# Attention output moved on chip to the expert products, and a new order for the first products

## The chip, the cores and the metric

The kernel runs on one core of one Trainium2 chip. The metric is the device time of one execution in microseconds (us), the median of the runs; lower is better. A core has TensorE (PE in the rows; its weight loads are PEld), VectorE (DVE), ScalarE (ACT), GpSimd (POOL), SyncE (SP) and 16 DMA engines. Each engine takes its instructions in the order in which the program lists them, and waits on semaphores for those of the others.

## The reference

Three stages follow each other. A delta-rule attention with a state of 48 x 48 for each of 4 x 8 heads goes over 768 tokens; its output, for 3072 tokens of 384 features, goes through 8 experts, all of which compute all tokens, weighted by a router whose weights are balanced by 8 Sinkhorn steps; a gated network with a 1024 x 1024 layer and an output layer ends it.

```python
# attention, per batch b and head h, over t
k_n = k / (norm(k) + 1e-6)
y[t] = q[t] @ state
state = state + beta[t] * outer(k_n[t], v[t] - k_n[t] @ state)
# experts; x is y as (3072, 384)
P = exp(x @ w_gate - max)
for _ in range(8):
    P /= P.sum(1) + 1e-9; P /= P.sum(0) + 1e-9; P *= N / E
out = sum_e P[:, e] * (relu(x @ w1[e]) @ w2[e])
# last network
((out @ m2_w1) * (out @ m2_w2)) @ m2_w3 @ m2_w_out
```

## The kernel before

The attention is worked in 12 chunks of 64 tokens for all 32 heads at once, 16 groups side by side on 128 partitions (two halves of 64, of which a feature-major tile like kt uses 48 rows). For each pair of chunks a triangular system is inverted on VectorE (`invert`, many short steps of lines L450, L651 and L663), from Gram products of the keys (`prep_k`, tile kt) that are copied to tile a0 and transposed (L637). For chunks 0 and 1 only the 16 x 16 blocks are inverted, and the rest is done by three corrections on TensorE (`substitute` makes R and tt; in `seq` the products of vs and tt, then three times R times u). `seq` carries the state from chunk to chunk (tiles u, st) and gives the chunk's output in xst; its feature-major form x, in two parts for exact fp32 products, is tile xr, which has two slots. `xload` brings it there: xst is written to xs_d in DRAM, read back into xst with features on 128 partitions, copied by ScalarE (line L443) into part 0 of xr, and the remainder by VectorE or GpSimd (L450) into part 1. From xr follow the router's logits (xr times wg) and the first expert's products (`e0`: xr times wA, then hA times wA, 72 products each for a chunk of 256 columns). After the last chunk come the Sinkhorn steps, and then the seven other experts (`phase_b`), which read xs_d again, and the last network (`phase_c`).

No order of instructions is written by hand. Each operation is recorded with its possible engines, a planned duration, what it reads and writes, and a priority (lower goes first); `Plan.order` then simulates the engines with these costs and fixes the order, and on which engine an operation runs where there is a choice. `room` gives buffers and PSUM banks, with a limit by class (attn 4 of 8). For TensorE there is a rule on fetching instructions: the planner reckons that a block of 256 instructions is ready `FETCH` = 4.4 us after the block before it was begun, and passes by an operation that would stand still for that. A random generator with a seed passes some attention operations by. Until the first expert product is planned, TensorE gets filler from 20 us on where nothing else can run: products of a zero tile wz (`fill`), which nobody reads. `lead` in the code is the next filler operation, and None once the filler is over. All loads and stores of this part are issued on SP's queue, which is in order too.

The loads at the start have priorities near -20, in the order kT of chunk 0 (with 16 rows of padding in each half, 512 KB), masks, kn of chunk 0, beta, kT and kn of chunk 1. Operations of chunk 0's chain have priorities of -131 to -129, those of the later chunks about -100, the first expert's products 200 and more.

```python
# xload before: one read back from DRAM, then the split
self.dma(raw, lambda: self.T["xs_d"][c].rearrange("h (k p) t -> p (h k) t", p=128), 393216, r, rk, pr, eng=q, lat=XLAT)
g.op({"ACT": act(768)}, lambda e: self.copy("ACT", dst(0), raw()), r=rk, w=[k(0)], prio=pr)
```

## Time and profile before

| what | value |
|---|---|
| runs | 1990.87, 1994.67, 1998.92 us |
| median | 1994.67 us |
| profiled execution | 1995.27 us, of which the span of the profile is 1993.5 us |
| TensorE busy | 1959.9 us (98%), granted clock 0.998 over the span |
| VectorE, ScalarE, GpSimd busy | 1576.1, 1043.6, 754.9 us |
| first product of xr and wA | 60.14 us |
| last copy of x into xr | 366.92 us |

The profile is one execution. TensorE's busy time holds the filler products, so it is read together with the rows of tile wz. The timeline merges instructions of one line that follow each other: the first number is the start, the second the length, and the brackets give the idle time before the group and what ended it.

### The profile page before, as it was taken

To read this page: it belongs to the slowest core of one execution; us is meant where nothing else is said; L and a number is where in the kernel's file an instruction comes from. 1 tells how busy PE (TensorE), PEld (TensorE's weight loads), DVE (VectorE), ACT (ScalarE), POOL (GpSimd) and SP (SyncE) were. 2 spreads that over 40 slices of the span, in tenths; PEclk is the share of its full clock that TensorE was granted. 3 is DMA by queue.
4 is the path that set the end of the run, shared out by engine and by line. 5 is a ranking of instruction groups with operands and counts; after the bars stand their busy time and mean duration, and the time that the engine had idled before them with its cause. 6 is when DMAs were issued, how large, how long until landed. Compare 5 with 4: busy or idle time off the path is not lost.

```text
span 1993.5 us, 41202 instructions
## 1 busy us (share of the span) xinstructions
PE 1959.9 (98%) x16054; PEld 1673.8 (84%) x16054; DVE 1576.1 (79%) x2753; ACT 1043.6 (52%) x2043; POOL 754.9 (38%) x964
## 2 busy tenths in 40 slices
PE   7999999999999999999999999999999999999999
PEld 6898889988888888888888888888888888888888
DVE  7989893588888787887788788888876776677875
ACT  6545433356555455544355455555554453676764
POOL 1201010457777666624433324334344533023310
PEclk9999999999999999999999999999999999999999
DMA  6443422266655565699999989999999989447341
GB/s 220 152 140 112 124 80 68 96 203 249 220 216 191 196 222 187 211 286 270 284 307 240 245 242 231 278 283 256 263 284 263 292 246 216 141 140 196 110 152 41
DMA packets 189636, 406.19 MB, mean 204 GB/s; under 512 B 16192, under 2 KB 112384, under 8 KB 175616
## 3 DMA queue, kind: packets, MB, share of 16 engines
q0 software_dynamic: 45792, 196.10, 36.8%
q1 hardware_dynamic: 143648, 207.45, 31.6%
q8 instruction: 126, 2.06, 0.4%
q14 instruction: 70, 0.57, 0.1%
HBM read 259.21 MB, written 144.28 MB: 202 GB/s over the span
## 4 chain that ended last, share of the span: by engine, by line
PE 86%; DVE 6%; DMA 4%; issue 2%; ACT 2%; POOL 1%; SPq 0%; POOLq 0%; ACTq 0%; DVEq 0%
PE b L439 86%; DMA wA<-wv_d 2%; DMA kt<-in_kT 1%; ACT rt L443 1%; DVE prod L450 1%; DVE b L450 1%; POOL xf_d L470 1%; DMA rt<-wo_d 0%; DVE p L453 0%; DMA rt<-w_d 0%; DVE hA L453 0%; DVE t L663 0%; DVE hB L453 0%; DVE acc L450 0%; DVE p L450 0%
## 5 line engine op out<-in xcount | busy, mean ns | idle before, releaser
L450 DVE TENSOR_TENSOR b<-b,rt 128x512 f32<-128x512 f32 x810 | 539.3, 694 | 104.3 <-ACT rt L443 99.8
L443 ACT ACTIVATE rt<-b 128x512 f32<-128x512 f32 x756 | 443.0, 603 | 314.6 <-PE b L439 241.8
L439 PE MATMUL b<-xT,wA 128*128 128x512 f32 x2028 | 518.6, 391 | 0.8 <-ACT rt L443 0.3
L439 PE MATMUL b<-hB,wA 128*128 128x512 f32 x1764 | 445.1, 390 | 4.3 <-DMA wA<-wv_d 1.6
L439 PEld LDWEIGHTS b<-xT,wA 128*128 128x128 f32 x2028 | 379.3, 188 | 79.9 <-DVE b L450 2.9
L439 PE MATMUL b<-hA,wA 128*128 128x512 f32 (+1 forms) x2124 | 441.8, 348 | 0.0
L439 PEld LDWEIGHTS b<-hB,wA 128*128 128x128 f32 x1764 | 330.4, 188 | 76.5 <-ACT hA L1267 4.1
L439 PEld LDWEIGHTS b<-hA,wA 128*128 128x128 f32 x2124 | 346.0, 189 | 51.3
L439 PE MATMUL b<-xr,wA 128*128 128x256 f32 (+1 forms) x1362 | 255.4, 326 | 0.8 <-DVE tt L450 0.5
L439 PEld LDWEIGHTS b<-xr,wA 128*128 128x128 f32 x1362 | 201.8, 190 | 21.8 <-DVE tt L450 0.7
L439 PE MATMUL b<-wS,wA 128*128 128x512 f32 x684 | 184.4, 391 | 0.4 <-ACT rt L443 0.3
L453 DVE SCALAR_TENSOR_TENSOR hA<-b,hA 128x512 fp32r<-128x512 f32 x188 | 126.9, 684 | 38.4 <-ACT hA L979 30.2
L470 POOL DMA_DIRECT2D xf_d<-acc x109 | 97.4, 896 | 139.7 <-DVE acc L450 106.2
L439 PEld LDWEIGHTS b<-wS,wA 128*128 128x128 f32 x684 | 127.7, 188 | 26.6 <-ACT rt L443 1.9
L450 DVE TENSOR_TENSOR tmp<-b,pb 128x512 f32<-128x512 f32 x129 | 89.1, 691 | 76.0 <-PE b L439 67.6
L453 DVE SCALAR_TENSOR_TENSOR hB<-b,hB 128x512 fp32r<-128x512 f32 x196 | 131.1, 686 | 3.0 <-ACT hB L1267 2.3
L1267 ACT ACTIVATE hB<-b 128x512 fp32r<-128x512 f32 x196 | 116.3, 603 | 21.6 <-PE b L439 14.7
L450 POOL TENSOR_TENSOR acc<-acc,tmp 128x512 f32<-128x512 f32 x78 | 102.3, 1312 | 45.5 <-DVE wA L450 20.8
L470 POOL DMA_DIRECT2D wA<-wf_d x56 | 31.7, 566 | 199.7 <-PE b L439 192.0
L1267 ACT ACTIVATE hA<-b 128x512 fp32r<-128x512 f32 x140 | 82.3, 610 | 39.6 <-PE b L439 36.0
L450 DVE TENSOR_TENSOR acc<-b,pb 128x512 f32<-128x512 f32 x81 | 55.9, 690 | 43.0 <-PE b L439 41.7
L470 POOL DMA_DIRECT2D xf_d<-tmp x65 | 57.2, 880 | 84.8 <-DVE tmp L450 49.4
(265 smaller groups left out, 2363.3 us busy)
## 6 DMA issues: line engine op xcount, KB each, us to landing
wA<-wf_d POOLq DMA_DIRECT2D x56, 1280.0 KB, 8.7
wA<-wv_d POOLq DMA_DIRECT2D x56, 768.0 KB, 8.7
wf_d<-wA SPq DMA_DIRECT2D x27, 1280.0 KB, 5.0
wA<-wc_d POOLq DMA_DIRECT2D x24, 1280.0 KB, 6.1
xf_d<-acc POOLq DMA_DIRECT2D x109, 256.0 KB, 5.5
wv_d<-wA SPq DMA_DIRECT2D x28, 768.0 KB, 4.1
xf_d<-tmp POOLq DMA_DIRECT2D x65, 256.0 KB, 5.6
yr<-in_moe_w SPq DMA_DIRECT2D x60, 192.0 KB, 2.5
```

The lines of the kernel that those rows point to most:

```text
L439: self.nc.tensor.matmul(*args, skip_group_check=True, **kw)
L443: self.nc.scalar.activation(out=out, in_=in_, func=AF.Copy, **({} if scale is None else {"scale": scale}))
L450: return self.E[eng].tensor_tensor(out=out, in0=in0, in1=in1, op=op)
L453: self.nc.vector.scalar_tensor_tensor(out=out, in0=in0, scalar=scalar, in1=in1, op0=op0, op1=op1)
L470: return self.g.op({eng: cost}, lambda _: e.dma_start(out=out(), in_=in_(), **({} if accum is None else {"accum_op": accum})), r=r, w=w, p ...
L1267: g.op({"ACT": actb(512)}, lambda e, s=s, hv=hv: nc.scalar.activation(out=hv(0), in_=self.ps(s, 512), func=AF.Relu), r=[s], w=[(o, 0, 0)], ...
```

## The change

`xload` no longer reads xs_d. Six transfers (`XMOVE`) take x from xst straight into part 1 of xr, and it is split in place; for chunk 0 three of the six are issued on ACT's queue. So that each transfer moves whole rows, the features lie in another order on the partitions: 96 of each 128 rows are two heads' features as they come, and the fourth pair of heads is spread over rows 96 to 127 of the three blocks. The rows of the gate and of the first expert's w1 are put in the same order before the launch. xs_d is still written, for the later experts, after the transfers in the program's order. kT and qT are loaded without the padding rows, each in two transfers, and the loads of chunks 0 and 1 stand in another order. In the planner, other attention products wait after 27 us (`HOLD`) until chunk 0's (`first`) are planned, the attention may hold two more PSUM banks before 44 us (`OPEN`), the fetch rule and the passing-by don't hold while filler lasts, several planned durations change, and so does the seed. Copies of chunk 1 into a0 and of chunk 0 into xst may go to VectorE. The filler products have 512 columns instead of 256, and half their number.

```diff
--- before.py
+++ after.py
@@ -37,10 +37,11 @@
-XLAT = 1.0
+XLAT = .6
+XMOVE = [(0, 0, D, 0, 0, 0, 3), (1, 0, D, D, 0, 0, 3), (0, 0, 32, 96, 0, 3, 1), (0, 32, 16, 96, 1, 3, 1), (1, 0, 16, 112, 1, 3, 1), (1, 16, 32, 96, 2, 3, 1)]
@@ -148,13 +149,15 @@
-    SEED = 79
+    SEED = 12
+    HOLD = 27.0
+    OPEN = 44.0
@@ -168,7 +171,9 @@
+        first = [o for o in self.ops if "PE" in o.engs and o.prio[0] <= -129 and o.ins >= 16]
+            o.end = None
@@ -245,7 +250,7 @@
-                if s.cls in g.caps and g.used.get(s.cls, 0) + need.get((g, s.cls), 0) >= g.caps[s.cls]:
+                if s.cls in g.caps and g.used.get(s.cls, 0) + need.get((g, s.cls), 0) >= g.caps[s.cls] + (2 if now < self.OPEN and s.cls == "attn" else 0):
@@ -292,6 +297,8 @@
+                if lead is not None and e == "PE" and o.ins >= 16 and now > self.HOLD and o.prio[0] > -125 and any(not x.end for x in first):
+                    continue
@@ -302,7 +309,7 @@
-                if o.low and full or e == "PE" and (fetch(o, now) > .1 or o.ins >= 16 and rng.random() < self.PASS_BY):
+                if o.low and full or e == "PE" and lead is None and (fetch(o, now) > .1 or o.ins >= 16 and rng.random() < self.PASS_BY):
@@ -466,7 +473,7 @@
-        cost = cost if eng == "SP" else 1.1
+        cost = 1.1 if eng == "POOL" else cost
@@ -491,7 +498,7 @@
-                  asys=((128, 1056), F32), t=((128, 1056), F32), prod=((128, NP, 1024), F32), xs=((128, 256), F32), bm2=((128, 2, 32), F32), wz=((128, 384), F16),
+                  asys=((128, 1056), F32), t=((128, 1056), F32), prod=((128, NP, 1024), F32), xs=((128, 256), F32), bm2=((128, 2, 32), F32), wz=((128, 640), F16),
@@ -504,7 +511,7 @@
-            self.dma(lambda nm=nm: T[nm], lambda src=src: a[src], 65536, [], [nm], -20.05 + i * .1)
+            self.dma(lambda nm=nm: T[nm], lambda src=src: a[src], 65536, [], [nm], -19.7 - i * .05)
@@ -536,8 +543,8 @@
-        for _ in range(400):
-            g.op({"PE": .107}, lambda e: self.mm(self.ps(sw, 256), T["wz"][:, 0:128], T["wz"][:, 128:384], start=True, stop=True),
+        for _ in range(200):
+            g.op({"PE": .214}, lambda e: self.mm(self.ps(sw, 512), T["wz"][:, 0:128], T["wz"][:, 128:640], start=True, stop=True),
@@ -550,9 +557,11 @@
-        self.dma(lambda: T["kn"][:, kn.at].rearrange("p g d -> p (g d)"), lambda: self.a["kn"][c], 393216, [], [kn], pr - 20 + c % 2)
+        self.dma(lambda: T["kn"][:, kn.at].rearrange("p g d -> p (g d)"), lambda: self.a["kn"][c], 393216, [], [kn], pr - 20.0 + (c % 2 if j else .1 * c), lat=0.0 if j else 1.3)
-        self.dma(lambda: T["kt"][:, k.at].rearrange("p g t -> p (g t)"), lambda: self.a["kT"][c], 524288, [], [k], pr - 20.1 + c % 2)
+        for b in range(2):
+            self.dma(lambda b=b: T["kt"][64 * b:64 * b + D, k.at].rearrange("p g t -> p (g t)"), lambda b=b: self.a["kT"][c, 64 * b:64 * b + D], 196608,
+                     [], [k if b else (k, b)], pr - 20.1 + (c % 2 if j else .25 * c), lat=0.0 if j else 1.3)
@@ -576,7 +585,7 @@
-        pg = pr if j == 0 else -120.0 + j if j > 1 else -99.5
+        pg = pr if j == 0 else -99.5 if j == 1 else -98.5 if j == 2 else -120.0 + j
@@ -594,17 +603,18 @@
+            ca = {"ACT": act(256, True), **({"DVE": dve(256)} if c == 1 else {})}
-            g.op({"ACT": act(256, True)}, lambda e, s=s, ss=ss, a0=a0: self.copy(
-                "ACT", T["a0"][:, a0.at, ss], self.ps(s, 8, 64)[:, :, 0:32], -1.0), r=[s], w=[ak], prio=pg)
+            g.op(ca, lambda e, s=s, ss=ss, a0=a0: self.copy(
+                e, T["a0"][:, a0.at, ss], self.ps(s, 8, 64)[:, :, 0:32], -1.0), r=[s], w=[ak], prio=pg)
-                g.op({"ACT": act(256, True)}, lambda e, s=s, ss=ss, a0=a0, r=r: self.copy(
-                    "ACT", T["a0"][r, a0.at, ss], self.ps(s, 8, 64)[r, :, 32:64], -1.0), r=[s], w=[ak], prio=pg)
+                g.op(ca, lambda e, s=s, ss=ss, a0=a0, r=r: self.copy(
+                    e, T["a0"][r, a0.at, ss], self.ps(s, 8, 64)[r, :, 32:64], -1.0), r=[s], w=[ak], prio=pg)
-                g.op({"ACT": act(128, True)}, lambda e, s=s, hf=hf, i=i: self.copy(
+                g.op({"ACT": act(128, True) + .08}, lambda e, s=s, hf=hf, i=i: self.copy(
@@ -644,11 +654,11 @@
-            g.op({"DVE": dve(4 * i * i) + .12}, port=True, fn=lambda e, pv=pv, i=i: self.tt(
+            g.op({"DVE": dve(4 * i * i)}, port=True, fn=lambda e, pv=pv, i=i: self.tt(
-            g.op({"DVE": dve(4 * i * i) + .11}, lambda e, pv=pv, i=i: nc.vector.tensor_reduce(
+            g.op({"DVE": dve(4 * i * i)}, lambda e, pv=pv, i=i: nc.vector.tensor_reduce(
@@ -791,7 +801,9 @@
-        self.dma(lambda: T["qt"][:, q.at].rearrange("p g t -> p (g t)"), lambda: self.a["qT"][c], 524288, [], [q], (pr if c > 1 else 2.5 + c) - 20)
+        for b in range(2):
+            self.dma(lambda b=b: T["qt"][64 * b:64 * b + D, q.at].rearrange("p g t -> p (g t)"), lambda b=b: self.a["qT"][c, 64 * b:64 * b + D], 196608,
+                     [], [q if b else (q, b)], (pr if c > 1 else 2.5 + c) - 20, lat=0.0 if c > 1 else 1.3)
@@ -813,14 +825,18 @@
-    def xload(self, dst, raw, rk, c, r, key, pr, q):
-
-        g = self.g
-        k = (lambda i: key[0:2] + (i,) + key[2:]) if isinstance(key, tuple) else lambda i: (key, i)
-        self.dma(raw, lambda: self.T["xs_d"][c].rearrange("h (k p) t -> p (h k) t", p=128), 393216, r, rk, pr, eng=q, lat=XLAT)
-        g.op({"ACT": act(768)}, lambda e: self.copy("ACT", dst(0), raw()), r=rk, w=[k(0)], prio=pr)
+    def xload(self, dst, src, c, r, key, pr, q):
+
+        g, T = self.g, self.T
+        raw = lambda: dst(1).bitcast(F32)
+        rk = [(key, "r", i) for i in range(len(XMOVE))]
+        for i, (b, e0, n, p0, kk, j0, nj) in enumerate(XMOVE):
+            self.dma(lambda p0=p0, n=n, kk=kk, nj=nj: T["xr"][p0:p0 + n, 1, key.at, :, kk:kk + nj].bitcast(F32).rearrange("p h k t -> p h (k t)"),
+                     lambda b=b, e0=e0, n=n, j0=j0, nj=nj: src()[64 * b + e0:64 * b + e0 + n, :, 128 * j0:128 * (j0 + nj)], 1024 * n * nj,
+                     r, rk[i:i + 1], pr, eng="ACT" if b and c == 0 else q, cost=.4, lat=XLAT)
+        g.op({"ACT": act(768)}, lambda e: self.copy("ACT", dst(0), raw()), r=rk, w=[(key, 0)], prio=pr)
-             r=rk + [k(0)], w=[k(1)], prio=pr)
+             r=[(key, 0)], w=[(key, 1)] + rk, prio=pr)
@@ -836,7 +852,7 @@
-            g.op({"ACT": .8}, scale, r=[("nv", 0)], w=[vk[i // 2]], prio=1.2 + c)
+            g.op({"ACT": .95}, scale, r=[("nv", 0)], w=[vk[i // 2]], prio=1.2 + c)
@@ -917,17 +933,14 @@
-            g.op({"ACT": act(512, True)}, lambda e, hf=hf: self.copy(e, T["xst"][:, xb.at, hf], self.ps(sy[hf], 512)),
+            g.op({"ACT": act(512, True), **({"DVE": dve(512)} if c == 0 else {})}, lambda e, hf=hf: self.copy(e, T["xst"][:, xb.at, hf], self.ps(sy[hf], 512)),
+        self.xload(lambda i: T["xr"][:, i, x.at].rearrange("p h k t -> p (h k) t"), lambda: T["xst"][:, xb.at], c, [(xb, 0), (xb, 1)], x, pr + .5, XQ)
-        xk = [("xs", c, b) for b in range(2)]
-        self.xload(lambda i: T["xr"][:, i, x.at].rearrange("p h k t -> p (h k) t"),
-                   lambda: T["xst"][:, xb.at].rearrange("p h f -> p (h f)")[:, 0:768].rearrange("p (k t) -> p k t", t=128), [(xb, "x")],
-                   c, xk, x, pr + .5, XQ)
@@ -1757,12 +1770,17 @@
+    d = np.arange(DM)
+    d = np.where(d % 128 < 96, d // 128 * 96 + d % 128, 288 + d // 128 * 32 + d % 128 - 96)
+    res["moe_w_gate"] = f(res["moe_w_gate"][d])
+    res["moe_w1"] = res["moe_w1"].copy()
+    res["moe_w1"][0] = res["moe_w1"][0][d]
```

## Rows read from the trace of the kernel before

**Rows 1.** The page: busy time, share and instructions of each engine.
```profile
PE 1959.9 (98%) x16054; PEld 1673.8 (84%) x16054; DVE 1576.1 (79%) x2753; ACT 1043.6 (52%) x2043; POOL 754.9 (38%) x964
```

**Rows 2.** Busy by stretch: length, PE, PEld, DVE, ACT, POOL, clock, DMA share, GB/s.
```profile
0.00:30.00 30.00, 18.98 (x450) 16.09 (x450) 19.05 (x41) 24.19 (x75) 2.09 (x12) 1.00 0.76 284
30.00:60.10 30.10, 27.13 (x748) 23.79 (x749) 26.01 (x45) 16.73 (x39) 9.15 (x6) 0.94 0.53 157
60.10:100.00 39.90, 38.72 (x1074) 35.15 (x1073) 37.26 (x54) 19.11 (x43) 9.99 (x7) 1.00 0.42 132
100.00:300.00 200.00, 195.62 (x5209) 180.29 (x5208) 183.27 (x286) 93.53 (x219) 20.27 (x17) 1.00 0.38 114
...
420.00:1993.50 1573.50, 1562.15 (x7015) 1306.36 (x7014) 1247.33 (x2205) 845.75 (x1583) 679.43 (x893) 1.00 0.77 226
```

**Rows 3.** Busy times by stretch, TensorE's products of tile wz alone.
```profile
30.00:60.10 30.10, 13.80 (x108) 0.94 0.53 157
```

**Rows 4.** Timeline, 10 to 16 us: start, us, engine, line, operation; idle before in brackets.
```profile
10.74 1.18 ACT L443 ACTIVATE a<-b 128x256 f32<-128x256 f32 x3
...
13.98 1.91 DVE L637 STREAM_TRANSPOSE asys<-a 128x1024 f32<-128x1024 f32 x1
...
15.19 1.14 PE L439 MATMUL b<-qt,kt 48*64 48x64 f32 x33 [1.38 <-issue]
```

**Rows 5.** Timeline, 31 to 37 us: update and first correction product of chunk 0.
```profile
31.76 1.76 PE L439 MATMUL b<-vs,tt 64*64 64x48 f32 x64
...
33.73 1.09 ACT L443 ACTIVATE xst<-b 128x512 f32<-128x512 f32 x2
...
34.94 0.91 ACT L443 ACTIVATE vs<-b 128x384 f32<-128x384 f32 x2
...
36.60 2.07 PE L439 MATMUL b<-vs,xst 64*64 64x48 f32 x64
```

**Rows 6.** Timeline of VectorE, 37 to 44 us, and the same line at 95 us.
```profile
37.83 0.56 DVE L450 TENSOR_TENSOR u<-b,vs 128x384 f32<-128x384 f32 x1 [0.27 <-ACT nrm L566]
...
40.95 1.73 DVE L576 TENSOR_TENSOR bm<-bm,nrm 128x32 f32<-128x32 f32 x1
...
42.61 1.01 DVE L450 TENSOR_TENSOR u<-b,vs 128x384 f32<-128x384 f32 x2
...
95.31 0.19 DVE L576 TENSOR_TENSOR bm<-bm,nrm 128x32 f32<-128x32 f32 x1
```

**Rows 7.** Timeline, 48 to 61 us: chunk 0's x from PSUM to the first expert product.
```profile
48.87 1.08 ACT L443 ACTIVATE xst<-b 128x512 f32<-128x512 f32 x2 [6.19 <-PE b L439]
...
49.98 1.77 SPq L470 DMA_DIRECT2D xs_d<-xst  x2
...
54.82 0.38 SPq L470 DMA_DIRECT2D xst<-xs_d  x1
...
57.96 0.84 ACT L443 ACTIVATE xr<-xst 128x768 fp32r<-128x768 f32 x1 [0.16 <-DMA xst<-xs_d]
...
60.14 0.60 PE L439 MATMUL b<-xr,wA 128*128 128x256 f32 x3
```

**Rows 8.** DMA issues: queue, count, KB each, median us from issue to landing.
```profile
xst<-xs_d SPq DMA_DIRECT2D x12, 384.0 KB, 3.5
...
y_d<-yr SPq DMA_DIRECT2D x36, 128.0 KB, 2.6
```

**Rows 9.** Timeline of TensorE, 89 to 93 us.
```profile
89.75 0.69 PE L439 MATMUL b<-asys,g 32*32 32x32 f32 x32 [1.13 <-DVE hA L453]
...
91.55 0.86 PE L439 MATMUL b<-xr,wg 128*16 128x256 f32 x6
```

**Rows 10.** Timeline, 366 us: x of chunk 11 into xr.
```profile
366.92 0.85 ACT L443 ACTIVATE xr<-xst 128x768 fp32r<-128x768 f32 x1 [2.64 <-PE b L439]
```

**Rows 11.** Timeline, 413 to 434 us: the loads of pb and their first use.
```profile
413.67 0.82 SPq L470 DMA_DIRECT2D pb<-p_d  x2
...
433.89 0.68 DVE L450 TENSOR_TENSOR acc<-b,pb 128x512 f32<-128x512 f32 x1
```

## The prediction

> **What bounds the kernel now.** I read the page first, then the busy times by stretch, then the timeline of the first 60 us, the waits there, and last the places where a delay could be hidden. TensorE is busy for 98% of the span [rows 1], but that figure counts filler. By stretch [rows 2], from 420 us on it stands idle for 11.4 of 1573.5 us: what happens there is a fixed amount of work, and only its start can move. From 60.1 us to 420 us it is idle for 8.3 us of 359.9, a little everywhere. The loose time is in front: in the first 30 us TensorE is idle for 11.0 us, and between 30.0 and 60.1 us it has 27.1 us busy, of which 13.8 us are products of the zero tile wz [rows 3]. So in 30.1 us before the first expert product there are 3.0 us idle and 13.8 us of filler: 16.8 us in which TensorE does nothing that is needed. The change speaks to this stretch, because the first expert product starts at 60.14 us [rows 7] when chunk 0's x has come on chip. The second thing to see in [rows 2] is VectorE: 37.3 of 39.9 us busy between 60.1 and 100 us and 183.3 of 200 us up to 300 us. While the attention runs there are nearly two bounds, and time given to TensorE alone isn't all kept.
>
> **The change part by part**, in the order of chunk 0's chain; each term is a gain in us.
>
> *Loads.* kT and qT lose the 16 padding rows of each half: 384 KB for 512 KB, in two issues for one. Keys kn of chunk 1 now go ahead of its kT, and VectorE may take some of chunk 1's six copies into a0. Ahead of chunk 1's kT go kT0, kn0, kn1 (3 x 384 KB) where masks, beta, kT0 and kn0 went (39 + 96 + 512 + 384 KB): its last byte comes at nearly the same place (1536 for 1543 KB). So the Gram product of chunk 1 stays near, and only ScalarE's and VectorE's work between it and the transpose at 13.98 us [rows 4] can shrink. In front of it lie six copies of 0.39 us on ScalarE [rows 4]; three of them moved would be 1.2 us at the most. Between 0 and 1.2, I take 0.6.
>
> *Costs in the planner* (scale 0.95 for 0.8, masked copies +0.08, the small inversion steps without +0.12). They move no work, they change who is put in front of whom. The rows show what that was worth: the update product of chunk 0 ends at 33.52 us, but ScalarE, still at other copies, gets to the copies of R at 33.73 and to those of vs at 34.94 us, and the first correction product starts at 36.60 us [rows 5]. With the two vs copies (0.46 each) at once on two engines after 33.7 us it would start near 34.4: 2.2 us. Between 0 and 2.2, I take 1.6: the new costs say by how much the old ones fell short on ScalarE (8 x 0.15 + 12 x 0.08 = 2.2 us), and most of these operations lie ahead of the two copies.
>
> *The hold* (after 27 us no other attention product on TensorE until chunk 0's are through). VectorE finished the first half of u at 38.39 us; the second could have followed the product, which ends at 38.67 us [rows 5], at about 38.9 us, but started at 42.61, because the norm of chunks 2 and 3 was ahead of it, with two products into bm of 1.18 and 1.73 us, the last of which [rows 6] took 0.19 us at 95.31. 3.7 us were lost. The hold binds TensorE, not VectorE, so this can come back: between 0 and 3.7, I take half, 1.9.
>
> *x path of chunk 0.* The two copies into xst take 1.08 us one after the other on ScalarE; on two engines 0.6: gain 0.5. They end at 49.95 us, and x is in hand for ScalarE at 57.96 [rows 7]: 8.0 us for a write to DRAM (two issues), its landing, a read and its landing. Now three issues on SP and three on ACT's queue go side by side, straight into xr. At 0.38 us an issue [rows 7] that is 1.14 us; no row shows a transfer from SBUF to SBUF. Nearest are the same bytes at 3.5 us and y_d<-yr at 2.6 us [rows 8]; the slow end is the first xs_d write, 4.84 us from its issue to the read that waited for it, and issues at half of 1.77 us each [rows 7]. So the new path takes 3.7 to 7.5 us, 4.6 by the nearest row; gain 3.4, between 0.5 and 4.3. ACT's three issues wait for both halves of xst, and behind them on ScalarE stand the copies of the state for chunk 1; that is 1.1 us at the most for a chain which doesn't set the first expert product, and I cost it at nothing.
>
> [...]
>
> *x path of the later chunks.* Six issues on SP (2.3 us) replace a read that waited for a write; gain near 1 us each, and hidden, since the x of chunks 2 to 11 has a chunk of products ahead of it. What moves is the place: before, x waited in xst, and the copy at 366.92 us went as soon as TensorE left the slot [rows 10]; now issue, landing and copies come after that, 2.3 + 3.5 us more. The work that hides it is the other slot's expert products. For chunk 11 the router and the Sinkhorn steps come that much later; the loads of pb are issued by 414.5 us, would be there at 419.3 even with the slow 4.84 us of above, and are used first at 433.89 us [rows 11]: 14 us of room. I cost it at nothing.
>
> *The rest.* The fetch rule is off while filler lasts, the filler has 512 columns and half the instructions, the attention may hold six PSUM banks before 44 us, the seed is another: no row gives these a price of their own, and I take 0, with the fetch rule as a rival. Some 84 more issues on SP are about 32 us of a queue that waits through most of 330 us: 0. The permuted rows of the gate and of the first expert's w1 are made before the launch.
>
> **The sum.** 0.6 + 1.6 + 1.9 = 4.1 us bring chunk 0's whole chain forward, the state for chunk 1 and VectorE's work with it: kept. The 0.5 + 3.4 = 3.9 us bring forward the expert products alone. They can take the place of filler [rows 3], but at 88.6 us TensorE has run dry (1.13 us) and chunk 1's router product is at 91.55 us [rows 9]: what it did early is missing there, unless chunk 1 too is early. I keep half, 2.0. Together 6.1 us of the profiled execution's 1995.27: 1989.2. That execution is 0.6 us above the median of the runs, so against the median 1994.67 it is 1988.6 us.
>
> **Rivals.**
> *All is kept*: the hold keeps VectorE free too and chunk 1 moves with chunk 0: 2.2 + 3.7 + 3.4 + 0.5 + 0.6 = 10.4 us, 1984.3. For it: 16.8 us of useless TensorE time stand there. Against it: the two dry places of [rows 9].
> *Nothing is kept*: VectorE is the bound until 100 us, TensorE idles in front of chunks 1 and 2 for what it gained: 1993 to 1996. For it: [rows 2].
> *Fetch stalls.* At 15.19 us TensorE stood 1.38 us for nothing that the profile shows, in the midst of one operation, with 33 of its 64 products still to come [rows 4]. The chain from the substitution to the state has seven operations of 64 products and 64 weight loads, 896 instructions; with 128 in each operation and a stop every other one, four stops of 1.38 us are 5.5 us: 1994. That can eat the gain, not turn it. [...]
> *Slower, by the late start of the moves.* From chunk 2 on, x leaves xst only when the slot in xr is free, and 5.8 us more pass before its products can start. It is covered while the other slot's products (144 of them, planned at 0.36 us for three: 17 us) and the attention last. If a chunk has less than that, TensorE waits; it decides at 0.6 us a chunk over ten chunks (6.1 us eaten), and makes 2005 at 1.6 us a chunk. SP stands in its queue for that slot, and the loads of the next chunks stand behind. For it: VectorE's 92%. Against it: at 366.92 us the copy came as the last of a row of products, with much left to do.
>
> **How the numbers follow.** A measurement of this kernel can tell 0.5%, 10 us, from no change: faster is below 1984.7, slower above 2004.6. Chances: the sum, 1985 to 1992, 0.52; all kept, 1979 to 1985, 0.21; nothing kept or fetch stalls, 1992 to 1999, 0.20; late moves, above 1999, 0.07, half of it above 2004.6 and half short of it, to which I add a little for an order that turns out badly elsewhere. Faster: 0.21 and the edge of the first case, 0.27; slower 0.06; the rest, 0.67. The terms by themselves reach from 0.2 us (0.5 x path, half kept) to 11.9 us (1.2 + 2.2 + 3.7 + 0.5 + 4.3), that is 1982.8 to 1994.4. With a little of the rivals on each side the range is 1981 to 1997.
>
> **What will show it.** The first product of xr and wA starts at 49 to 54 us, not at 60.14. From the end of the copies into xst to ScalarE's copy into xr pass 4 to 5.5 us, not 8.0. The second u starts within 1 us of its product. Filler between 30 us and the first expert product falls by 4 us or more. Between 60 and 130 us TensorE has 2 us more idle than now. From 420 us to the end the length stays within 3 us, as the work there is the same. Wrong it would be if the first expert product is early and the end isn't (the give-back is whole), if TensorE waits for transfers into xr, or if idle time without a releaser grows in chunk 0's chain.

## The result, and the profile after

The kernel after takes 2021.47 us (median of 4 runs, 2018.58 to 2023.6) against 1994.79 us for the kernel before (four runs too, one more than in the table above): ratio 1.0137, 95% interval 1.0122 to 1.0152. It is 27 us slower; 6 us faster was forecast, and the range ended at 1997. The profiled execution is 2020.77 us with a span of 2019.0 us.

The busy times by stretch come first, in the order of [rows 2] (length, PE, PEld, DVE, ACT, POOL, clock, DMA share, GB/s); the last row has TensorE alone.

```profile
0.00:30.00 30.00, 14.87 (x386) 12.72 (x387) 13.79 (x33) 18.77 (x56) 2.09 (x12) 1.00 0.98 245
60.10:100.00 39.90, 36.52 (x869) 32.71 (x859) 31.58 (x44) 20.14 (x42) 12.78 (x7) 0.96 0.48 134
100.00:300.00 200.00, 187.81 (x4813) 172.25 (x4813) 166.37 (x267) 89.86 (x214) 19.78 (x18) 0.97 0.36 103
300.00:400.00 100.00, 95.32 (x1853) 88.94 (x1851) 50.17 (x81) 30.44 (x65) 5.30 (x6) 1.00 0.22 60
400.00:450.00 50.00, 48.75 (x360) 45.91 (x361) 42.00 (x88) 26.65 (x51) 35.67 (x28) 1.00 0.39 120
...
445.00:2019.00 1574.00, 1561.99 (x7015) 1.00 0.77 226
```

The reader reads it from the end. The last 7015 products of TensorE take 1574.0 us, from 445.0 us on; before, the last 7015 took 1573.5 us, from 420.0 us on [rows 2]. The tail is the same work at the same speed, and it begins 25.0 us later. All of the loss lies ahead of it. From 60.1 to 450 us TensorE is busy 36.52 + 187.81 + 95.32 + 48.75 = 368.4 of 389.9 us, idle for 21.5. Before, the rows for the same stretch are these:

```profile
300.00:400.00 100.00, 98.76 (x1423) 94.82 (x1422) 45.04 (x96) 34.96 (x71) 22.54 (x23) 1.00 0.27 83
400.00:450.00 50.00, 48.52 (x275) 42.16 (x274) 44.16 (x81) 28.79 (x54) 26.09 (x32) 1.00 0.63 210
```

With [rows 2] that is 38.72 + 195.62 + 98.76 + 48.52 = 381.6 us busy, idle for 8.3. So 13.2 us more are idle. From 60.1 us to the start of the tail, the kernel before first and after second (length, PE, clock, DMA share, GB/s):

```profile
60.10:420.00 359.90, 351.61 (x7844) 1.00 0.35 105
60.10:445.00 384.90, 363.39 (x7869) 0.98 0.33 95
```

It is nearly the same number of products, and 25.0 of the 25.5 us by which the span grew: 13.2 us of idle time (21.5 for 8.3) and 11.8 us by which TensorE is busy longer. By an estimate, at most two thirds of the second part go to the clock column: 0.96 over 39.9 us and 0.97 over 200 us are some 1.6 + 6.0 = 7.6 us of a clock that before stood at 1.00 there, if all work went in step with it. The products of xr and wA took 415 ns each (median) in the kernel after at a clock of 0.50, from 66 to 68 us, and 282 ns at 1.00, from 71 to 78 us. The first expert product comes 3.5 us later, but that is no term of its own: by 60.1 us both kernels have about as many products behind them, filler left out (1024 before, 1017 after).

The late first product is read in the timeline of the kernel after (start, us, engine, line, operation; idle before in brackets):

```profile
21.93 0.38 SPq L477 DMA_DIRECT2D wgr<-in_moe_w_gate  x1
...
31.08 0.18 DVE L523 CAST wg<-wgr 128x24 fp32r<-128x24 f32 x1 [6.76 <-DMA wgr<-in_moe_w_gate]
...
39.74 1.10 PE L446 MATMUL b<-vs,tt 64*64 64x48 f32 x64
...
41.95 2.07 PE L446 MATMUL b<-vs,xst 64*64 64x48 f32 x64
...
43.98 0.97 DVE L457 TENSOR_TENSOR u<-b,vs 128x384 f32<-128x384 f32 x2
...
50.72 1.73 DVE L585 TENSOR_TENSOR bm<-bm,nrm 128x32 f32<-128x32 f32 x1
52.37 0.55 DVE L457 TENSOR_TENSOR u<-b,vs 128x384 f32<-128x384 f32 x1
...
52.97 0.88 PE L446 MATMUL b<-u,kraw 64*48 64x48 f32 x59 [1.99 <-DVE u L457]
...
55.45 1.08 ACT L450 ACTIVATE xst<-b 128x512 f32<-128x512 f32 x2
...
56.56 3.55 SPq L477 DMA_DIRECT2D xr<-xst  x3
56.56 2.07 ACTq L477 DMA_DIRECT2D xr<-xst  x3
...
62.78 0.84 ACT L450 ACTIVATE xr<-xr 128x768 fp32r<-128x768 f32 x1 [1.07 <-DMA xr<-xst]
...
63.67 0.39 PE L446 MATMUL b<-xr,wA 128*128 128x256 f32 x1 [0.31 <-ACT xr L450]
```

The update product of chunk 0 starts at 39.74 us; before it was 31.76 [rows 5]. Chunk 0's chain is eight us late by then. VectorE stands 6.76 us in the midst of chunk 0's inversion for a load of the gate's weights, which was issued at 21.93 us and is at hand at 31.08. Behind 39.74 us the chain is faster than before: 23.9 us to the first expert product instead of 28.4.

The waits of TensorE up to the first expert product say what else was late (engine, line, for what: us in total, times, longest), after and then before:

```profile
PE b L446 <- DMA kt<-in_kT: 11.3, 7, 4.4
PE b L446 <- issue: 6.5, 4, 1.7
```

```profile
PE b L439 <- DMA kt<-in_kT: 6.7, 2, 4.6
PE b L439 <- issue: 1.4, 1, 1.4
```

Between 60 and 440 us ScalarE's copies into xr wait for the moves:

```profile
ACT xr L450 <- DMA xr<-xst: 30.2, 12, 5.6
```

TensorE itself waits there for the three engines' copies into xr for 6.6 us (0.8 for ScalarE's, 3.9 for GpSimd's, 1.9 for VectorE's), and for 4.5 us for nothing that the profile shows; before it was none and 1.1.

At the start 11.3 us of waiting are for kT, 4.6 more than before. The loads tell why: two stretches of 5 us, the kernel after in the first fence, the kernel before in the second (length, PE, clock, DMA share, GB/s).

```profile
7.50:12.50 5.00, 3.16 (x88) 1.00 1.08 197
...
17.50:22.50 5.00, 0.63 (x12) 1.00 1.04 219
```

```profile
7.50:12.50 5.00, 3.50 (x120) 1.00 1.03 406
...
17.50:22.50 5.00, 4.28 (x88) 1.00 1.05 389
```

The DMA engines are as busy in both, at a share above 1.0, and move half as much in these two stretches (from 12.5 to 17.5 us, in between, it is 349 GB/s for 412). What differs is the shape: the kernel after loads kT and qT as transfers of 48 rows, before they had 128; kn, kraw and vs have 128 in both. By the order of issue, the four transfers of qT of chunks 0 and 1 are under way here:

```profile
9.50:12.50 3.00, 2.43 (x84) 1.00 1.02 188
```

That is 188 GB/s at a share of 1.02. Why transfers into 48 rows move so much less no run shows; what the shape costs is tried below.

### The profile page after: what moved, and what is told of

It is laid out like the page before. It is cut to its first block, busy times and chain, and to the rows that moved or that the text cites. A ratio compares the mean times of both kernels' runs of the same rounds, so it can differ in the third digit from the quotient of the medians.

```text
span 2019.0 us, 41131 instructions
## 1 busy us (share of the span) xinstructions
PE 1966.5 (97%) x15933; PEld 1671.2 (83%) x15933; DVE 1571.9 (78%) x2754; ACT 1042.0 (52%) x2045; POOL 754.9 (37%) x961
## 4 chain that ended last, share of the span: by engine, by line
PE 85%; DMA 5%; DVE 4%; ACT 2%; SPq 1%; issue 1%; POOL 0%; ACTq 0%; POOLq 0%; DVEq 0%
PE b L446 85%; SPq L477 1%; DMA kt<-in_kT 1%; DMA xr<-xst 1%; DMA wA<-wv_d 1%; ACT rt L450 1%; DMA yr<-in_moe_w 1%; DVE b L457 1%; DVE hA L460 0%; DMA rt<-wo_d 0%; DMA rt<-w_d 0%; DMA qt<-in_qT 0%; DVE p L460 0%; ACT xr L450 0%; DMA kn<-in_kn 0%
## 5 line engine op out<-in xcount | busy, mean ns | idle before, releaser
L446 PE MATMUL b<-hA,wA 128*128 128x512 f32 (+1 forms) x2313 | 497.1, 352 | 5.4 <-DMA wA<-wv_d 1.8
L446 PEld LDWEIGHTS b<-hA,wA 128*128 128x128 f32 x2313 | 381.1, 189 | 68.1 <-ACT hB L1280 3.3
L446 PE MATMUL b<-hB,wA 128*128 128x512 f32 x1575 | 392.4, 389 | 0.0
L446 PEld LDWEIGHTS b<-hB,wA 128*128 128x128 f32 x1575 | 295.6, 188 | 61.4
L446 PE MATMUL b<-xr,wA 128*128 128x256 f32 (+1 forms) x1362 | 260.0, 331 | 2.2 <-issue 1.2
L446 PEld LDWEIGHTS b<-xr,wA 128*128 128x128 f32 x1362 | 206.8, 195 | 23.2 <-issue 1.5
L460 DVE SCALAR_TENSOR_TENSOR hA<-b,hA 128x512 fp32r<-128x512 f32 x209 | 140.3, 686 | 47.1 <-ACT hA L992 44.4
L1280 ACT ACTIVATE hB<-b 128x512 fp32r<-128x512 f32 x175 | 102.6, 611 | 50.3 <-PE b L446 44.9
L460 DVE SCALAR_TENSOR_TENSOR hB<-b,hB 128x512 fp32r<-128x512 f32 x175 | 117.1, 683 | 8.1 <-ACT hB L1280 7.5
L457 POOL TENSOR_TENSOR acc<-acc,tmp 128x512 f32<-128x512 f32 x78 | 103.3, 1324 | 44.7 <-DVE wA L457 20.7
L1280 ACT ACTIVATE hA<-b 128x512 fp32r<-128x512 f32 x161 | 95.8, 602 | 17.1 <-PE b L446 10.9
```

The costliest lines, as they stand in the source:

```text
L446: self.nc.tensor.matmul(*args, skip_group_check=True, **kw)
L457: return self.E[eng].tensor_tensor(out=out, in0=in0, in1=in1, op=op)
L460: self.nc.vector.scalar_tensor_tensor(out=out, in0=in0, scalar=scalar, in1=in1, op0=op0, op1=op1)
L1280: g.op({"ACT": actb(512)}, lambda e, s=s, hv=hv: nc.scalar.activation(out=hv(0), in_=self.ps(s, 512), func=AF.Relu), r=[s], w=[(o, 0, 0)], ...
```

## The experiments

Each of them was timed against the kernel before on the chip that it ran on; several chips were used, so ratios are compared and not times. Two kinds must be kept apart. In some the instructions keep the order of before or of after on every engine, so that little else than the edit changes. In the others the planner draws a new order, and the order is part of what is measured. *Idle* is TensorE's idle time from 60.1 to 450 us, summed as above; *x waits* is the time for which ScalarE's copies into xr stand waiting for a transfer, 60 to 440 us.

| kernel | order | ratio, interval | first expert product | idle | x waits |
|---|---|---|---|---|---|
| before | | 1 | 60.14 | 8.3 | 4.8 |
| after | new | 1.0137 [1.0122, 1.0152] | 63.67 | 21.5 | 30.2 |
| b_narrow | of before | 1.0025 [1.001, 1.0041] | 62.57 | 8.8 | 6.4 |
| b_movefix | of before | 1.0303 [1.0282, 1.0323] | 58.96 | 40.2 | 60.0 |
| b_move01 | of before | 1.0009 [0.9996, 1.0022] | 58.38 | 10.1 | 6.3 |
| a_wide | of after | 1.0093 [1.0066, 1.0119] | 58.77 | 20.5 | 30.3 |
| a_wgr | of after | 1.0138 [1.0105, 1.0172] | 62.45 | 21.8 | 29.9 |
| a_dramfix | of after | 1.0095 [1.0073, 1.0117] | 63.63 | 16.9 | 26.6 |
| a_dram | new | 1.0076 [1.0048, 1.0103] | 64.97 | 14.0 | 7.8 |
| a_wdram | new | 1.0072 [1.0045, 1.0099] | 61.73 | 14.9 | 7.0 |
| a_fetch | new | 1.0119 [1.0098, 1.014] | 64.30 | 21.2 | 27.0 |
| a_seed79 | new | 1.0179 [1.0154, 1.0204] | 63.15 | 27.8 | 33.3 |
| b_move | new | 1.0132 [1.0096, 1.0168] | 60.31 | 22.2 | 30.6 |
| b_seed12 | new | 1.0055 [1.0039, 1.0071] | 63.21 | 13.8 | 4.6 |
| b_seed1 | new | 1.0152 [1.0133, 1.017] | 63.43 | 23.3 | 7.5 |
| b_seed2 | new | 1.0036 [1.0024, 1.0049] | 58.39 | 12.5 | 2.6 |
| a_honest | new | 1.0083 [1.0054, 1.0113] | 56.34 | 15.6 | 5.4 |
| a_honest79 | new | 1.0045 [1.0029, 1.0061] | 58.35 | 9.6 | 7.7 |
| a_hw79 | new | 1.0085 [1.0072, 1.0099] | 55.68 | 13.9 | 7.9 |
| a_hybrid79 | new | 1.0088 [1.0074, 1.0101] | 55.44 | 16.9 | 2.3 |

The last three columns are of one execution each; that of a_seed79 is 8 us above its median, that of a_honest79 3 us below, that of b_move01 5 us below.

**The loads.** First theory: the transfers of 48 rows are slow, and the loss is theirs. Rival: it is the late place of the gate's load, wgr. `a_wide` loads kT and qT in the order of after, but each half as 512 columns of all 128 partitions, padding included:

```diff
-lambda b=b: T["kt"][64 * b:64 * b + D, k.at].rearrange("p g t -> p (g t)"), lambda b=b: self.a["kT"][c, 64 * b:64 * b + D]
+lambda b=b: T["kt"][:, k.at].rearrange("p g t -> p (g t)")[:, 512 * b:512 * b + 512], lambda b=b: self.a["kT"][c][:, 512 * b:512 * b + 512]
```

> The changed kernel with its order of instructions unchanged; only kT and qT are again loaded on all 128 partitions, padding included, in two transfers of half the columns each. Theory of the narrow loads (a transfer to 48 partitions runs at half the rate): the first 25 us move 350 GB/s or more instead of 245, VectorE no longer waits 6.8 us for wgr, the first expert product comes at 55 to 58 us instead of 63.7, and the time falls by 5 to 15 us, to 2006 to 2016. Theory of the moves and theory of the order: the first expert product may come earlier, but the end stays within 4 us of 2021, since the loss is made later.

`a_wgr` issues the load of wgr right behind that of the masks:

```diff
         order = self.g.order()
+        order.remove(self.wgr_op)
+        order.insert(order.index(self.masks_op) + 1, self.wgr_op)
```

> The changed kernel with its order of instructions unchanged, but for the load of wgr, which SP issues right behind masks. Theory of the narrow loads: the 6.8 us wait is gone, the slow loads are still there; the first expert product comes at 56 to 59 us and the time falls by 3 to 8 us. Theories of the moves and of the order: the end stays within 4 us of 2021.

`b_narrow` is the reverse of the first, in the order of before:

```diff
-self.dma(lambda: T["kt"][:, k.at] ..., lambda: self.a["kT"][c], 524288, [], [k], pr - 20.1 + c % 2)
+for b in range(2):
+    self.E["SP"].dma_start(out=T["kt"][64 * b:64 * b + D, k.at] ..., in_=self.a["kT"][c, 64 * b:64 * b + D])
```

> The kernel before with its order of instructions unchanged; each load of kT and qT is made by two transfers of 48 rows instead of one of 128. Theory of the narrow loads: the DMA share stays near 1 until about 30 us instead of 24, the first expert product is 3 to 8 us later and the time grows by 3 to 12 us, to 1998 to 2007. Theories of the moves and of the order: within 3 us of 1995.

With full loads the first expert product comes at 58.77 us, 4.9 earlier, and the whole is 0.44% better than after. The first 30 us of a_wide, to be read beside the first line of the section above (284 GB/s at a share of 0.80 for 245 at 0.98):

```profile
0.00:30.00 30.00, 17.30 (x395) 13.02 (x396) 19.31 (x42) 22.59 (x69) 2.10 (x12) 0.77 0.80 284
```

It is early although TensorE's granted clock was 0.82 from 10 to 20 us and 0.50 from 20 to 30 us of this execution, where after had 1.00. What lowered it no run shows: here the engine was busy for 1.5 of 5 us from 12.5 to 17.5 us, and in after for 0.63 of 5 us from 17.5 to 22.5 us, at a clock of 1.00 there and up to 30 us. With wgr early VectorE no longer waits for it, and the first expert product comes 1.2 us earlier, but nothing is gained in the total: the update product of chunk 0 still starts at 40.02 us. In b_narrow the two symptoms appear in a kernel that did not have them. Its first 30 us by stretch:

```profile
0.00:30.00 30.00, 18.99 (x422) 15.34 (x422) 14.83 (x37) 23.59 (x74) 2.10 (x12) 0.94 0.96 246
```

And VectorE's wait in its timeline:

```profile
28.44 0.18 DVE L516 CAST wg<-wgr 128x24 fp32r<-128x24 f32 x1 [4.10 <-DMA wgr<-in_moe_w_gate]
```

246 GB/s at a share of 0.96 stand where [rows 2] have 284 at 0.76. So the narrow loads cost 0.25% (5 us) in the order of before and 0.44% (9 us) in that of after (by the two intervals 0.1 to 0.4 and 0.1 to 0.75%), and wgr is their symptom: it is issued at 21.15 us in b_narrow and at 14.16 before. It is a part of the 27 us and not the larger one: a_wide has an early first product and is still 0.93% slower than before.

**The moves.** `a_dram` takes x through DRAM again and `a_wdram` undoes the narrow loads as well, each with a new order; `b_move` puts the moves alone into the kernel before, with a new order.

```diff
-self.xload(..., lambda: T["xst"][:, xb.at], c, [(xb, 0), (xb, 1)], x, pr + .5, XQ)   # six moves
+self.xload(..., [(xb, "x")], c, xk, x, pr + .5, XQ)                                   # xs_d, written and read back
```

> The changed kernel with the old path of x (write to xs_d, read back into xst, old row order), planned anew. Theory of the moves (six slow issues a chunk, x late in xr): most of the loss goes, 1998 to 2006. Theory of the narrow loads: the first expert product is still after 62 us, the time 2015 to 2025. Theory of the order: anything from 2005 to 2025, without a pattern in the waits for xr.

> The changed kernel with both kinds of transfer undone: kT and qT on 128 partitions (two transfers of half the columns), x by way of xs_d; planned anew. What is left of the change is the planner's part (hold, banks, fetch rule, durations, seed, filler, order of the first loads). Theory that the transfers cost more than the planner reckons, and nothing else: 1990 to 1998. Theory of the order (the planner's part loses time by itself): 2003 to 2012.

> The kernel before with the direct moves of x alone (with the new row order, planned at 0.4 us an issue as in the change, three issues on ACT for chunk 0), planned anew with its old seed. Theory of the moves: slower by 6 to 15 us, 2001 to 2010, with TensorE waiting for xr. Otherwise: the prediction's 3.9 us for chunk 0's path would show, 1990 to 1996.

The first two are 0.6% better than after (12 us), the third loses 26 us, more than either of its theories had. In a_wdram both kinds of transfer are undone, and what is left of the change is the planner's part with its seed, and the order of the first loads: 0.72% (14 us), half of the whole loss, are still there. But every new order is a draw of its own, so the moves were also put into the order of before as it stands. `b_movefix` replaces the read by a place holder and issues the moves at ScalarE's copy, where the plan has the slot in xr free (for chunks 0 and 1, whose slots are free from the start, ahead of the write of xs_d):

```diff
-self.dma(raw, lambda: self.T["xs_d"][c]..., 393216, r, rk, pr, eng=q, lat=XLAT)
-g.op({"ACT": act(768)}, lambda e: self.copy("ACT", dst(0), raw()), r=rk, w=[k(0)], prio=pr)
+g.op({"SP": .5}, lambda _: None, r=r, w=rk, prio=pr, nbytes=393216, lat=XLAT)
+def split(e):
+    if c > 1:
+        self.moves(c)
+    self.copy("ACT", dst(0), raw())
+g.op({"ACT": act(768)}, split, r=rk, w=[k(0)], prio=pr)
```

> The kernel before with its own order kept instruction for instruction on every engine; only chunk 0 to 11's read of xs_d is replaced by the six direct moves (for chunks 0 and 1 issued ahead of the xs_d writes, from chunk 2 on issued where ScalarE's copy into xr stands, that is when the slot is free), features and weight rows permuted to match. Theory A (the moves themselves cost: six issues and a landing, 6.1 us, now stand between the freed slot and the first product of each chunk, and loads queue behind them): first expert product near 58.5 us, but TensorE waits for xr from chunk 2 on, 0.8 us a chunk or more, ratio 1.004 to 1.008. Theory B (it is the newly drawn order that costs, and with an unchanged order the moves are hidden): ratio 0.998 to 1.002, waits of TensorE for xr under 2 us in 60 to 420 us.

It is 59 us slower (2053.49), far more than either theory had. ScalarE's waits for x between 60 and 440 us, first in b_movefix, then in the kernel before:

```profile
ACT xr L444 <- DMA xr<-xst: 60.0, 10, 8.6
```

```profile
ACT xr L443 <- DMA xst<-xs_d: 4.8, 5, 1.9
```

The x of chunk 7, again in b_movefix and then in before:

```profile
281.02 3.82 SPq L836 DMA_DIRECT2D xr<-xst  x6
...
286.26 0.84 ACT L444 ACTIVATE xr<-xr 128x768 fp32r<-128x768 f32 x1 [7.27 <-DMA xr<-xst]
287.13 0.60 ACT L999 ACTIVATE hA<-b 128x512 fp32r<-128x512 f32 x1
290.50 0.87 ACT L444 ACTIVATE u<-b 128x384 f32<-128x384 f32 x2 [2.77 <-PE b L440]
```

```profile
242.21 0.38 SPq L470 DMA_DIRECT2D xst<-xs_d  x1
...
259.37 0.84 ACT L443 ACTIVATE xr<-xst 128x768 fp32r<-128x768 f32 x1 [2.12 <-PE b L439]
```

Before, the read of chunk 7 is issued 17 us ahead of the copy and has a place to land, xst. The moves land in xr itself and can't begin until TensorE leaves the slot. Their six issues take 3.82 us, the landing follows, and ScalarE stands for 7.27 us, with the copies of hA and of u behind it in its queue, and after them those of yr and of the state st. Over ten copies it stands for 6.0 us on the mean (0.5 to 8.6). In six of the ten chunks SP stands for TensorE's products before the moves, 45.3 us in all, and these copies have 44.7 of the 60.0 us. In the other four (chunks 2, 3, 4 and 6) the profile names no such wait; most of what they cost is in chunks 4 and 6 (13.3 us), whose moves stand behind other issues of SP because the edit puts them at ScalarE's copy. So b_movefix shows more than the price of a late slot alone. Before, the reads of chunks 2 to 6 stood only 3 to 7 us ahead of their copies. TensorE's waits of 60 to 440 us are then for ScalarE's xr (14.4 us), for VectorE's hA (6.8), for ScalarE's g, u and yr (5.0, 4.4 and 3.8). By stretch, its busy time falls to 180.06 of 200 us from 100 to 300 us, and the mean granted clock is 0.91, where it was 1.00 before.

```profile
100.00:300.00 200.00, 180.06 (x4456) 163.83 (x4454) 155.42 (x253) 82.11 (x194) 15.23 (x13) 0.91 0.33 98
...
400.00:450.00 50.00, 44.75 (x321) 42.71 (x321) 21.14 (x42) 15.89 (x31) 16.49 (x17) 0.87 0.31 98
```

`a_dramfix` tries the other side: the order of after, with its moves left out and x read back from xs_d as soon as that is written.

```diff
-self.dma(lambda ...: T["xr"][p0:p0 + n, 1, key.at, ...], lambda ...: src()[...], ..., r, rk[i:i + 1], pr, cost=.4, lat=XLAT)
+g.op({e: .4}, lambda _: None, r=r, w=rk[i:i + 1], prio=pr, nbytes=1024 * n * nj, lat=XLAT)
...
+def readx(self, c, xb):
+    self.nc.sync.dma_start(out=self.T["xst"][:, xb.at]..., in_=self.T["xs_d"][c].rearrange("h (k p) t -> p (h k) t", p=128))
...
+                if b:                      # behind the second write of xs_d
+                    self.readx(c, xb)
```

> The kernel after with its own order kept on every engine; the six moves of each chunk are left out and x is brought by the old path, xs_d written and read back into xst, the read issued right behind the write, so that x waits in xst for its slot as before; weight rows in plain order. Theory A (the moves between the freed slot and the first product are the larger part of after's loss): 10 to 20 us better than after, 2001 to 2011 us, although chunk 0's x comes 1.5 us later; ScalarE's waits for DMA in its copies into xr fall from 30 us to under 12. Theory B (the order itself, drawn anew on wrong costs, is the loss, and it was planned around the moves): within 5 us of after, 2016 to 2026 us.

The ratio of 1.0095 lies between the two theories, and the waits did not go: 26.6 us are left. The timeline of a_dramfix shows why the edit did not do what it was meant to do; ScalarE's copies into xst end at 248.61 us:

```profile
248.63 0.85 SPq L945 DMA_DIRECT2D xs_d<-xst  x2
...
252.76 0.38 SPq L841 DMA_DIRECT2D xst<-xs_d  x1
...
256.52 0.84 ACT L450 ACTIVATE xr<-xst 128x768 fp32r<-128x768 f32 x1 [3.71 <-DMA xst<-xs_d]
```

In the order of after x itself is ready late: the write follows its copies at once, and write, read and landing take 7.9 us to ScalarE's copy. 0.42% (8 us; by the two intervals 0.15 to 0.7%) come back though most of the waits stay. Whether more would come back without them is not shown.

In the kernel after, too, most moves start as soon as x is ready. Its chunk 2:

```profile
121.84 1.08 ACT L450 ACTIVATE xst<-b 128x512 f32<-128x512 f32 x2 [1.42 <-PE b L446]
122.95 5.04 SPq L477 DMA_DIRECT2D xr<-xst  x6
...
129.35 0.84 ACT L450 ACTIVATE xr<-xr 128x768 fp32r<-128x768 f32 x1 [1.43 <-DMA xr<-xst]
```

For chunks 0 to 6 the moves are issued within 0.1 us of the end of the copies into xst, so the slot is free; ScalarE's copy stands 5.9 to 6.4 us behind that end, where the plan counts some 4.1 us (six issues of 0.4 us, then 1.7 us until the last bytes have landed and are signalled), and waits 17.2 of its 30.2 us there. Only in chunks 7 to 11 do the moves start late, 6.7 to 26 us behind the copies, after SP has stood for TensorE's products; these five have 13.0 us of the waits.

`b_move01` moves only chunks 0 and 1, whose slots are free, in the order of before; the others are read from DRAM, in four transfers because of the permuted rows.

```diff
+                if b == 0 and c < 2:
+                    self.moves(c)
...
+for a, n, p in ((0, 288, 96), (288, 96, 32)) if c > 1 else ():
+    for h in range(2):
+        self.nc.sync.dma_start(out=..., in_=self.T["xs_d"][c][h, a:a + n].rearrange("(k p) t -> p k t", p=p))
```

> The kernel before with its own order; only chunks 0 and 1, whose slots in xr are free from the start, are moved directly; the later chunks are read from DRAM as before, in four transfers for one because of the permuted rows. If a direct move is a gain wherever the slot is free and a loss where it isn't: first expert product 1 to 2 us earlier than before (58 to 59 us), no wait of ScalarE for the later chunks beyond before's, and the total -2 to 0 us against before, ratio 0.9985 to 1.0015. If the earlier start of chunk 0's products upsets the order behind it: over 1.002.

The first expert product is 1.8 us earlier (58.38) and the total is that of before (1.0009, the interval holds 1). The profiled span is 1993.5 us, the same as before, in one of its faster executions. TensorE's timeline at the place of [rows 9], in b_move01:

```profile
88.91 0.69 PE L440 MATMUL b<-asys,g 32*32 32x32 f32 x32 [1.14 <-DVE hA L454]
```

The dry place of 1.13 us before is there again, and idle time between 60.1 and 450 us has grown by 1.8 us: what chunk 0 gains is given back whole, as far as this can be measured.

**The order.** Each kernel here changes the seed, and nothing else of the kernel before or after.

```diff
-    SEED = 79
+    SEED = 12      # b_seed12; 1 in b_seed1, 2 in b_seed2; a_seed79 is the reverse, in the kernel after
```

> The kernel before with the changed kernel's seed and nothing else: how much an order drawn anew moves the time by itself. If the order is a small matter: within 4 us of 1995. If any new order costs what the old seed had been chosen to avoid: 2000 to 2015.

> The kernel before with seed 1 for 79 and nothing else. Theory A (any order that is drawn anew is worse, since the one of before was the best of many for this chip): ratio 1.003 to 1.008, like the 1.0055 of seed 12, with the same signs: more idle time of TensorE between 60 and 420 us. Theory B (seed 12 alone is a bad draw): ratio 0.998 to 1.002.

> The kernel before with seed 2 for 79 and nothing else: a third new draw of the same plan. If the seed of before is one of the best of many draws: ratio 1.004 to 1.018, as seeds 12 (1.0055) and 1 (1.0152). If the draws lie on both sides: 0.992 to 1.002.

> The kernel after with the old seed 79 in place of 12, all else as after. If the order's luck is what after lost, another draw moves it either way: seed 12 was a bad draw for after if this runs under 2014 us. If it stays at 2016 to 2028 us, the seed is only noise of a few us on top, and what the plan takes for granted (loads at 300 GB/s, 0.4 us a move) is the larger part for every draw.

With no other change the kernel before loses 0.36, 0.55 and 1.52% by another seed; the last is more than either theory for it had. Its worst draw has the same marks as the kernel after, here 100 to 300 us of b_seed1:

```profile
100.00:300.00 200.00, 184.05 (x4837) 168.41 (x4834) 154.66 (x258) 81.18 (x189) 15.60 (x12) 0.89 0.36 110
```

Less busy (184.05 us for 195.62 in [rows 2]), and a lower granted clock (0.89 for 1.00). So three draws of three are worse than the order of before, and the seed that is good there is no better in the kernel after (1.0179).

`a_fetch` puts the fetch rule and the passing-by back while filler lasts:

```diff
-e == "PE" and lead is None and (fetch(o, now) > .1 or ...)
+e == "PE" and (fetch(o, now) > .1 or ...)
```

> The kernel after with the fetch rule and the passing-by in force while filler lasts, as before; everything else as after, planned anew. If fetch stalls are what the start lost, idle time without a releaser before the first expert product falls from about 8 us to under 5 us and that product comes 2 us earlier or more, near 61 us; in the total at most 3 us better than after, 2016 to 2024. If not, the idle time without a releaser stays and the total stays within 5 us of after.

TensorE's idle time without a releaser before the first expert product is 3.2 us instead of 6.5, and that product comes no earlier (64.30). Before, it was 1.4 us. So the stops have grown with the change, but halving them brought the product no earlier. That instruction fetch makes them, in blocks of 256 instructions, is the planner's reckoning; no run shows it. The total is 0.2% better, with intervals that overlap.

**The plan's prices.** `a_honest` and `a_honest79` keep all of after, and let the planner reckon with what the trace showed of the moves and of the narrow loads:

```diff
-XLAT = .6
+XLAT = 1.2
-    eng="ACT" if b and c == 0 else q, cost=.4, lat=XLAT)
+    eng="ACT" if b and c == 0 else q, cost=.75, lat=XLAT)
-    ... self.a["kT"][c, 64 * b:64 * b + D], 196608,      # and qT
+    ... self.a["kT"][c, 64 * b:64 * b + D], 360000,
```

> The changed kernel, its transfers as they are, but planned with what they were seen to take: an issue of the direct moves at 0.75 us for 0.4, 0.6 us more to their landing, and the narrow loads at 360000 bytes for 196608. Theory that the loss comes from an order planned with costs that the chip does not honour: the waits for xr and wgr go, 2000 to 2010. Theory that the transfers themselves cost the time: 2015 to 2025, whatever the plan.

> The kernel after with seed 79 and measured costs in the plan: 0.75 us a move for 0.4, landing 1.2 for 0.6, kT and qT loads reckoned as 360 KB for 196 KB. Before it stand 2028 us for seed 79 with after's own costs, and 2010 us for seed 12 with the measured costs. If the plan's wrong costs are a loss for every draw: 2005 to 2018 us. If the 12 us of seed 12 were the luck of one draw: 2020 to 2035 us.

Seed 12 gains 0.54% over after (1.0083 for 1.0137), seed 79 1.3% (1.0045 for 1.0179). The wait for wgr is gone in both. The prices of moves and loads were changed together, so these runs don't tell them apart. ScalarE's waits for x in a_honest79:

```profile
ACT xr L450 <- DMA xr<-xst: 7.7, 5, 3.7
```

And its busy times from 100 to 300 us:

```profile
100.00:300.00 200.00, 195.84 (x5124) 179.51 (x5123) 175.51 (x285) 86.98 (x205) 17.06 (x16) 0.98 0.37 100
```

The moves are the same transfers; only the order differs, and with it what ScalarE does while they are under way. Last, `a_hw79` adds the full-width loads (reckoned at their 262144 bytes) to the measured prices of the moves, and `a_hybrid79` besides sends chunks 2 to 11 through DRAM.

```diff
+        if c < 2:
             self.xload(..., lambda: T["xst"][:, xb.at], c, [(xb, 0), (xb, 1)], x, pr + .5, XQ)
...
+        if c > 1:
+            g.op({"SP": 2.0}, read, r=[("xs", c, b) for b in range(2)], w=[(xb, "x")], prio=pr + .5, nbytes=393216, lat=1.0)
```

> The kernel after with seed 79, kT and qT loaded on all 128 partitions in two halves of columns, and the moves planned at 0.75 us an issue and 1.2 us to land. If narrow loads and wrong costs add up as measured one by one (5 us and 12 to 25 us), it comes to 1996 to 2003 us, level with the kernel before or up to 0.4% slower. If another draw decides: 2004 to 2020 us.

> As a_hw79, but from chunk 2 on x comes through DRAM as before (four reads, planned at 2.0 us of the queue), and only chunks 0 and 1 are moved directly. If the late moves still cost something at their measured price: 2 to 8 us better than a_hw79, with ScalarE's waits for x under 6 us in 60 to 440 us; at best 1988 to 1995 us, a little better than the kernel before. If a plan that knows their price hides them: the two within 4 us of each other, the difference being the draw.

Both have the first expert product at 55.4 to 55.7 us, the earliest of all, and both are 0.85 to 0.88% slower than before. They are within 1 us of each other: as far as two draws can show it, moves that are planned at their price cost no more than the way through DRAM. a_hw79 is 0.4% (8 us) worse than a_honest79 though its loads are faster (278 GB/s for 243 over the first 30 us); a new draw can make that much, as the seeds above show. No version beat the kernel before.

## Why the prediction was wrong

**The later chunks' moves, "I cost it at nothing".** This step failed in its mechanism. The prediction saw that issue and landing would come after the slot is free, and gave them 5.8 us; ScalarE's waits in b_movefix are 6.0 on the mean. It named the other slot's expert products as the work that hides them, and so asked only whether TensorE had something to do. The copy that waits is ScalarE's, and behind it stand the copies of hA, u, yr and st, which TensorE's products read. In b_movefix, where the order does not cover them, the moves cost 59 us. In the kernel after the late slot is the smaller part of these waits (13.0 of 30.2 us); the larger is the time of the moves themselves, which the plan had priced too low. The rival "slower, by the late start of the moves" was the right mechanism with the wrong queue, and had a chance of 0.07. Its evidence against, the copy of 366.92 us [rows 10], was one copy of one chunk.

**Issues at 0.38 us.** That was taken from a plain read [rows 7]. The moves on SP take 0.6 us each (3.8 us for six, up to 5.0), and 1.2 us on SP for chunk 0, where SP and ACT issue at once (56.56 to 60.11 us for three; ACT's own three took 2.07). The new path of chunk 0, from the end of the copies into xst to ScalarE's copy, took 6.25 us, inside the stated 3.7 to 7.5 and not the 4.6 chosen; gain 1.8 of 3.4 us. The 0.5 us for copies into xst on two engines did not come: both stayed on ScalarE (55.45 us, 1.08).

**The loads, "its last byte comes at nearly the same place (1536 for 1543 KB)".** Bytes were counted and the rate was not asked. The rate falls to 188 to 219 GB/s in stretches with such loads, for 389 to 406 before, and a gain of 0.6 us became a loss of 5 to 9.

**"the seed is another: no row gives these a price of their own, and I take 0".** The absence of a row was taken for the absence of a cost. Three other seeds cost the kernel before 7 to 30 us. The rows that could have warned are [rows 2]: 8.3 us idle in 359.9 us of work in a fixed order on four engines is little, and an order drawn anew has more to lose than to win.

How the 27 us divide can't be settled by adding these up, since the order is planned around the other two. What is shown: with full loads in the same order, 0.44% back; with the old path in the same order, 0.42% back; the rest, about 0.5%, is no more than another seed takes. With both undone and a new order, 0.72% are left (a_wdram). So about half of the loss, by this run, lies in the planner's part and its draw, where the prediction counted gains of 1.6 and 1.9 us and nothing for the rest; how much of it is the seed, the hold, the banks or the changed costs was not tried. Six kernels with a move priced at 0.4 us (after, a_fetch, a_seed79, b_move, and a_wide and a_wgr, which keep after's order) have x waits of 27 to 33 us and ratios of 1.0093 to 1.0179; the six that price it as measured or have no late move (a_honest, a_honest79, a_hw79, a_hybrid79, a_dram, a_wdram) have 2 to 8 us and 1.0045 to 1.0088. The waits lie far apart; the ratios do not overlap, but their intervals do (a_wide from 1.0066, a_honest up to 1.0113). And b_seed1, which has no move at all, stands at 1.0152, so a ratio alone does not tell a bad price from a bad draw; the waits do. That wrong prices, of moves and loads together, make the waits is shown by two pairs with the seed held (30.2 to 5.4 us, 33.3 to 7.7), each with a new order. Whether a good order with the moves exists was not tried.

**The costs in the planner, 1.6 us, and the hold, 1.9.** The hold did its first step: both parts of u follow the product at once (43.98 us, product until 44.02). And it came back, as the text feared: the two products into bm are now in front of the last u, and TensorE waits 1.99 us there. The chain from the update product on became 4.5 us shorter, hold, costs and x path together, which is less than the 1.6 + 1.9 + 3.9 of the sum and was lost in front of it. How it divides between hold and costs no run shows.

**Kept or given back.** Half of an early first product was to be kept. b_move01, in the order of before, has it 1.8 us early and keeps nothing that can be measured; a_honest, a_honest79, a_hw79 and a_hybrid79, in new orders, have it 1.8 to 4.7 us early and are slower all the same. Of what the profile was to show, two things came true: the second u, and the length from the end of the attention on (1574.0 for 1573.5 us). Most of the others did not: filler between 30 us and the first expert product is 13.37 us for 13.80. Two signs that it was wrong, by its own list, are there: TensorE waits 6.6 us for the copies into xr that stand behind the moves, and idle time without a releaser before the first expert product grew from 1.4 to 6.5 us.

## What to carry to other kernels

Ask of a transfer which buffer it lands in: one that has a place of its own can be issued long before (in the kernel before the read of chunk 7, 17 us ahead of its copy), one that lands in the reader's slot starts when the slot is free, and its whole length then stood here in the queue of the engine that reads it first (7.27 us for chunk 7 in b_movefix). Price a transfer in the plan at what a trace shows of its own shape (here 0.60 us an issue for a move, 0.38 for a read), and a load by rows as well as by bytes (188 to 219 GB/s with 48 rows, 389 to 406 with 128). And where a planner draws the order, a change of seed or of a cost is a change of the kernel (three seeds cost 0.36 to 1.52%): hold the order to measure a part, and measure a few draws of the unchanged kernel before a gain of 1% is promised.
